# Regrouping v's projection weights on GpSimd, and projecting v by full-width matmuls

## The chip, the core and the metric

The kernel runs on one core of one Trainium2 chip, with one launch. The time is that of the device, in microseconds; a result is the median of several executions. Engines are named as in the profile: PE (TensorE, with PEld for its weight loads), DVE (VectorE), ACT (ScalarE), POOL (GpSimd) and SP (SyncE, which here only issues DMAs).

## The reference

Two independent parts are computed on 2048 tokens of width 576, and laid side by side in the output. Part A is a local attention with 32 heads of 18 elements and a window of 8 positions, 2 apart. Part B is a gated long convolution (short taps on k, times v, a convolution as long as the sequence, times q).

```python
# part A
qkv = (x @ wqkv).reshape(B, S, 3, H, Dh)               # H = 32, Dh = 18
logits = einsum("bhsd,bhswd->bhsw", q, kg) * scale     # kg, vg: k, v at s - 2w, w = 0..7
o = einsum("bhsw,bhswd->bhsd", softmax(logits), vg)
a = o.reshape(B, S, D) @ wo
# part B
kv = (sum over t of k_pad[t:t + S] * shift_k[:, 3 - t]) * v
b = q * (irfft(rfft(kv) * rfft(ssm_k)) + kv * ssm_D)
```

## The kernel before

**Layout.** Part A works with features on the partitions. `project(comp, jj)` makes q, k and v (comp 0, 1, 2) from the transposed x: output features in four tiles of 128 (ct 0 to 3) and one of 64 (ct 4), tokens in two halves of 1024 (jj). The 576 input features are contracted as four blocks of 128 (`body`, kb 0 to 3, lines 360 and 364) and a tail of 64 (`tails`, lines 371 and 377). One unit of work is a tile for 512 of its tokens; two units fill a two-bank PSUM tile, which ACT evacuates (line 394).

**The order of v's features.** q and k are wanted in the order of the weights. v and the attention output are wanted in another: feature a + 9 n of the matrix (a = 0 to 8, n = 0 to 63) stands in row n of group a, so that a column tile holds two groups a of 64 features. Head h has features 18 h to 18 h + 17, so row n then belongs to head n // 2, which lets softmax weights be spread over partitions by one DMA. The kernel gets this order when it loads weights into PE: `wa(kb, a)` is a view of 64 columns of v's weights with a step of 9 elements. Each of them makes a matmul over 64 columns of the array, and two of these, at column positions 0 and 64, fill one PSUM tile.

**The work around it.** VectorE first makes the taps of part B for four blocks of 512 tokens (`taps`, lines 558 to 562), while PE projects q and k, folds finished blocks (`mirror`, line 570) and folds the filter (`fold_filter`, line 615). Then come the logits (DVE products line 745, head sums on PE line 754), softmax (lines 773 to 789), the weighted sums of v (line 846 and PE line 862 or 876), and the output projection; the spectra of part B (lines 589 and 692) are filled in between, and its products and inverse transform (lines 985, 1006, 1038) end the kernel.

**What sets the order.** The program is scheduled by hand. Matmul work lies in a queue `units`; at marked points `until()` takes the next few, a count from the list `PLACES`, so that PE's order is fixed when the kernel is built, with the help of a planner's clocks (`pe`, `dve`) that use constants. v's nine units are interleaved with the spectra of x by the list `FXS`. Every engine takes its instructions in their order.

**Places the change touches.** `xw` holds the transposed x and the weights; `w_at` says where. `Ks` is a large scratch tile that holds angles of the sine tables early on and filter spectra later. `load_w` issues three DMAs of one third of wqkv on SP's queue: one of 512 rows, and two of the last 64, once for each half of the partitions. It already takes another target in `to`. The third for v is loaded in the loop over the taps at i = 1, between the filter's transposing loads. POOL builds constants at the start (lines 212 to 295), and later issues DMAs, among them those of `fold_filter` (line 620).

Of the kernel before, what the change touches and what calls it, by code (L numbers as in the profile page):

```python
# [31 lines left out]
def view(t, offset, dims):  # L32

    return bass.AP(tensor=t.tensor, offset=t.offset + offset, ap=[list(t.ap[0])] + [list(d) for d in dims])
# [3 lines left out]
def kernel(  # L38
# [13 lines left out]
    nc = tc.nc  # L52
    Bsz, S, D = A_x.shape
# [42 lines left out]
    def bank2(name, tag):  # L96
        return pp.tile([128, 2, 512], FP32, name=name, tag=tag)
# [6 lines left out]
    xw = main.tile([128, 12 * HB], BF16, name="xw")  # L104
# [11 lines left out]
    def xT(kb, t0, n):  # L116
        return view(xw, HB * (3 + 3 * (t0 // 1024)) + 1024 * kb + t0 % 1024, [[1, n]])

    def x5(jj):
        return view(xw, HB * (3 + 3 * jj) + 4096, [[1, 512]])  # L120

    def w_at(kb, comp):
        return HB * (9, 10, 5)[comp] + D * kb if kb < 4 else 11 * HB + D * (1, 2, 0)[comp]

    def wq(kb, comp, c0, n):
        return view(xw, w_at(kb, comp) + c0, [[1, n]])

    def wa(kb, a):

        return view(xw, w_at(kb, 2) + a, [[9, 64]])  # L130

    def load_w(eng, comp, to=None):
        low, high = (to[:, 0:4, :], to[:, 4, :]) if to is not None else \
            (view(xw, w_at(0, comp), [[D, 4], [1, D]]), wq(4, comp, 0, D))
        eng.dma_start(low, A_wqkv[0:512, comp * D:(comp + 1) * D].rearrange("(kb p) a -> p kb a", p=128))
        for r in range(2):
            eng.dma_start(high[64 * r:64 * r + 64, :], A_wqkv[512:576, comp * D:(comp + 1) * D])
# [25 lines left out]
    Ks = main.tile([128, 12 * HB], BF16, name="Ks")  # L163
# [3 lines left out]
    def k_at(m, part):  # L167
        return 3 * HB * (3 - m) + HB * part

    def kTok(m):  # L170
        return view(Ks, k_at(m, 2), [[D, 4], [1, D]])
# [24 lines left out]
    def load_v(i):  # L196
        vt = sp1.tile([128, 4, D], BF16, name="vt", bufs=2)
        nc.sync.dma_start(vt[0:128:2], vf[BL * i:BL * i + 256, :].rearrange("(p c) d -> p c d", c=4))
        nc.sync.dma_start(vt[1:128:2], bass.AP(tensor=vf.tensor, offset=vf.offset + (BL * i + 256 + 3) * D,
                                              ap=[[4 * D, 64], [-D, 4], [1, D]]))  # L200
        vts.append(vt)

    def load_filter(m):

        m = NBL - 1 - m
        nc.sync.dma_start_transpose(kTok(m), B_ssm_k[:, BL * m:BL * m + BL])
# [62 lines left out]
    for c0, p0, p1 in ((0, 0, 128), (128, 0, 128), (256, 0, 128), (384, 0, 128), (512, 0, 64), (512, 64, 128)):  # L269
        EHS.append(main.tile([128, 32], BF16, name=f"E{len(EHS)}"))  # L270
        e = EHS[-1][p0:p1, :]
# [43 lines left out]
    def pe(us, tag, evac, ready=0.0, first=True, last=True):  # L315

        clk["P"] = max(clk["P"], ready, psum[tag].popleft() if first else 0.0) + us
        clk["A"] = max(clk["A"], clk["P"] + 0.1) + evac
        if last:
            psum[tag].append(clk["A"])  # L320
        return clk["A"]
# [8 lines left out]
    def until():  # L330

        for _ in range(next(places, 0)):
            if units:
                p = max(clk["P"], psum["A"][0] if psum["A"] else 0.0)
                pop(next((n for n, u in enumerate(units) if len(u) < 4 or u[3] <= p), 0))
# [13 lines left out]
    def dest(comp, ct):  # L349
        if comp == 0:  # L350
            return q, (ct * S if ct < 4 else 4 * S), 0
        return (k if comp == 1 else v), (ct * KW if ct < 4 else 4 * KW), PAD


    def project(comp, jj):
        def body(ps, ct, jj, jp, first):
            for kb in range(4):
                se = dict(start=(kb == 0 and not first), stop=(kb == 3 and first))
                if ct < 4 and comp < 2:
                    nc.tensor.matmul(ps[:, jp, :], wq(kb, comp, 128 * ct, 128), xT(kb, 1024 * jj + 512 * jp, 512), **se)  # L360
                    continue
                for e in range(2):
                    w = wa(kb, min(2 * ct + e, 8)) if comp == 2 else wq(kb, comp, 512, 64)
                    nc.tensor.matmul(ps[64 * e:64 * e + 64, jp, :], w, xT(kb, 1024 * (jj if ct < 4 else e) + 512 * jp, 512),  # L364
                                     tile_position=(0, 64 * e), **se)

        def tails(ps, ct, jj, first):
            se = dict(start=first, stop=not first)
            if ct < 4 and comp < 2:
                for r in range(2):  # L370
                    nc.tensor.matmul(ps[:, r, :], wq(4, comp, 128 * ct, 128)[64 * r:64 * r + 64],  # L371
                                     x5(jj)[64 * r:64 * r + 64], tile_position=(64 * r, 0), **se)
                return
            for e in range(2):
                w = wa(4, min(2 * ct + e, 8)) if comp == 2 else wq(4, comp, 512, 64)
                for r in range(2):
                    nc.tensor.matmul(ps[64 * e:64 * e + 64, r, :], w[64 * r:64 * r + 64],  # L377
                                     x5(jj if ct < 4 else e)[64 * r:64 * r + 64], tile_position=(64 * r, 64 * e), **se)

        def unit(ct, jj, jp, first, box):  # L380
            t, o, pad = dest(comp, ct)
            if jp == 0:
                box["ps"] = bank2("ps_proj", "A")
                if first:
                    tails(box["ps"], ct, jj, True)
            ps = box["ps"]
            body(ps, ct, jj, jp, first)
            if jp == 0:
                clk["P"] += 1.15 if first else 0.9
                return  # L390
            if not first:
                tails(ps, ct, jj, False)
            pe(0.9 if first else 1.15, "A", 1.02)
            nc.scalar.activation(view(t, o + pad + 1024 * jj, [[512, 2], [1, 512]]), ps[:], ACT.Copy)  # L394
            if ct == 4 and comp > 0:
                nc.scalar.dma_start(view(t, o, [[1, PAD]])[64:128, :], view(t, o + 1024, [[1, PAD]])[0:64, :])

        for ct in range(4) if jj < 2 else [4]:
            first = ct % 2 == 1 if ct < 4 else comp == 1
            box = {}  # L400
            for jp in range(2):
                units.append((0.9 + 0.25 * (jp != first), partial(unit, ct, jj % 2, jp, first, box),
                              f"v{jj}{ct}" if comp == 2 else f"proj{comp}"))
# [149 lines left out]
    def taps(i):  # L553
        kj, vt = kjs[i], vts[i]
        kv = kv_of(i)
        for j in (3, 2, 1, 0):
            o = kv if j == 3 else sp1.tile([128, 4, D], BF16, name="tB")[:]
            dve(2304, lambda: nc.vector.tensor_tensor(  # L558
                o, kj[:, 3 - j:7 - j, :], skb[:, 3 - j, :].unsqueeze(1).to_broadcast([128, 4, D]), ALU.mult))
            if j < 3:  # L560
                dve(2304, lambda: nc.vector.tensor_tensor(kv, kv, o, ALU.add))  # L561
        return dve(2304, lambda: nc.vector.tensor_tensor(kv, kv, vt[:], ALU.mult))
# [85 lines left out]
    def add_half(t, to, of):  # L648
        nc.gpsimd.dma_start(half(t, to), half(t, of), accum_op=ALU.add, max_dma_last_dim=HB)

    def turn_filter(m):
        for part in range(2):
            add_half(Ks, k_at(m, part), k_at(m - 1, part))

    for i in range(NBL):
        r = taps(i)
        until()
        if i < 2:
            load_k(i + 2)
            load_v(i + 2)  # L660
        if i == 1:
            load_filter(0)
            load_w(nc.sync, 2)
            for m in range(1, NBL):
                load_filter(m)
        if i == 1:
            nc.scalar.preload_act_table_set("natural_log_exp_and_others")
            nc.scalar.activation(warm[:], pib[:], ACT.Exp)
        rest = [units.popleft()] if i == 3 and units and getattr(units[0][1], "args", ())[2:3] == (1,) else []
        for n in range(2):  # L670
            units.insert(3 * n, (0.5, partial(mirror, i, n), "x"))
        if i == 3:
            units.extendleft([fold_filter(m) for m in (3, 2)][::-1] + rest)
# [456 lines left out]
    for n, (j, t, i) in enumerate(todo):  # L1130
# [5 lines left out]
        if i == j and t == 2 and j < NBL - 1:  # L1136
            a, b = inverse(j, 0, HD, r), inverse(j, HD, HD, r)
# [40 lines left out]
```

## Time and profile before

| | |
|---|---|
| time, median of 3 runs | 221.6 us (221.13 to 221.75) |
| the profiled execution | 221.13 us, of which the span is 219.4 us |
| PE busy | 206.3 us (94%) |
| DVE busy | 200.3 us (91%) |
| ACT busy | 151.6 us (69%) |
| POOL busy | 48.9 us (22%) |
| granted PE clock | full speed in all but the last stretch (0.99) |

Times of single instructions are counted from the start of the span. A row of a timeline gives start, length, engine, line, operation, output and input, and count of merged instructions; a bracket says how long the engine had idled before it and what ended that. PE's matmuls overlap, so a group's length in the chain of waits says more than the sum of its matmuls.

### The profile page before, as it was taken

Reading aid. Unit: us, or ns where it says so; the run is one execution under the profiler, and the core shown is the slowest. Engines: PE = TensorE matmul, PEld = TensorE weight load, DVE = VectorE, ACT = ScalarE, POOL = GpSimd, SP = SyncE. Lnnn points to the kernel's source line nnn. Section 1 sums busy time; section 2 is a strip of 40 time slices with the busy share of each in tenths; the row PEclk is TensorE's granted clock in tenths of the full one; section 3 lists DMA queues with packets and bytes.
Section 4 is the critical chain, followed back from the end, with each engine's and each line's share of the span. In section 5 each row is a group of like instructions: output and inputs, shape, how many; then the busy total and the mean of one; then the engine's idle time right before and its main releaser. Section 6 shows DMA issues by size and latency. Waiting matters only on the chain.

```text
span 219.4 us, 5341 instructions
## 1 busy us (share of the span) xinstructions
PE 206.3 (94%) x2262; PEld 119.1 (54%) x2266; DVE 200.3 (91%) x159; ACT 151.6 (69%) x218; POOL 48.9 (22%) x93
## 2 busy tenths in 40 slices
PE   7999899999699999999999999999979999999891
PEld 3543344444455556565576777555546666666560
DVE  7969999999989949899898699999999999999982
ACT  3699766896686799965359888755487776756530
POOL 8989800000320206220640000000240001130000
PEclk9999999999999999999999999999999999999999
DMA  6999987999150035999999485481282103580034
GB/s 211 269 282 276 266 286 253 158 200 253 28 87 4 0 54 82 189 178 221 226 249 236 59 232 133 68 183 55 74 249 74 40 4 108 172 251 13 3 100 115
DMA packets 32295, 32.59 MB, mean 149 GB/s; under 512 B 17136, under 2 KB 28016, under 8 KB 32272
## 3 DMA queue, kind: packets, MB, share of 16 engines
q1 hardware_dynamic: 25902, 21.93, 41.2%
q0 software_dynamic: 3744, 7.82, 17.8%
q10 hardware_dynamic: 2626, 2.52, 3.4%
q8 instruction: 17, 0.28, 0.5%
q14 instruction: 6, 0.05, 0.1%
HBM read 13.11 MB, written 4.72 MB: 81 GB/s over the span
## 4 chain that ended last, share of the span: by engine, by line
PE 72%; ACT 15%; DVE 7%; issue 3%; DVEq 0%; ACTq 0%
PE ps_proj L364 10%; PE ps_proj L360 7%; PE ps_acc L862 7%; PE ps_wo L915 6%; PE ps_z L1006 6%; PE ps_inv L1038 5%; PE ps_fx L692 4%; PE ps_log L754 4%; PE ps_fk L589 3%; PE ps_proj L482 3%; ACT Ks L635 2%; ACT xw L695 2%; PE ps_rev L615 2%; ACT qk L394 2%; PE ps_proj L377 2%
## 5 line engine op out<-in xcount | busy, mean ns | idle before, releaser
L745 DVE TENSOR_TENSOR av<-qk 128x4096 bf16<-128x4096 bf16 (+1 forms) x20 | 40.5, 2074 | 4.3 <-PE ps_log L754 4.2
L360 PE MATMUL ps_proj<-xw 128*128 128x512 bf16 x93 | 22.6, 380 | 0.8 <-ACT qk L394 0.5
L364 PE MATMUL ps_proj<-xw 128*64 128x512 bf16 x176 | 23.0, 396 | 0.0
L1019 ACT ACTIVATE av<-ps_z 128x768 bf16<-128x768 f32 x23 | 17.4, 809 | 5.3 <-PE ps_z L1006 5.3
L695 ACT ACTIVATE xw<-ps_fx 128x576 bf16<-128x576 f32 x32 | 18.5, 665 | 2.0 <-PE ps_fx L692 2.0
L974 POOL DMA_DIRECT2D TB<-in_B_q_dram x4 | 3.0, 742 | 75.7 <-DVE qk L846 45.4
L635 ACT ACTIVATE Ks<-ps_fk 128x576 bf16<-128x576 f32 x32 | 18.3, 660 | 1.7 <-PE ps_fk L590 1.5
L394 ACT ACTIVATE qk<-ps_proj 128x1024 bf16<-128x1024 f32 x14 | 14.4, 1027 | 7.0 <-PE ps_proj L371 3.7
L364 PEld LDWEIGHTS <-xw 128*64 128x64 bf16 x176 | 14.7, 180 | 7.3 <-issue 5.2
L915 PE MATMUL ps_wo<-qk 128*128 128x288 bf16 x128 | 18.1, 287 | 0.4 <-ACT qk L866 0.4
L692 PE MATMUL ps_fx<-xw,TB 64*128 64x288 bf16 x256 | 17.8, 283 | 0.2 <-ACT xw L571 0.2
L589 PE MATMUL ps_fk<-Ks,TB 128*128 128x384 bf16 x64 | 17.2, 327 | 0.1
L394 ACT ACTIVATE v<-ps_proj 128x1024 bf16<-128x1024 f32 x9 | 9.2, 1025 | 11.4 <-PE ps_proj L377 7.0
L561 DVE TENSOR_TENSOR xw<-xw,tB 128x2304 bf16<-128x2304 bf16 x12 | 16.3, 1358 | 0.4
L1038 PE MATMUL ps_inv<-av,TI 128*128 128x288 bf16 (+1 forms) x112 | 16.1, 292 | 0.6 <-ACT av L1019 0.6
L558 DVE TENSOR_TENSOR tB<-kj,skb 128x2304 bf16<-128x2304 bf16 x12 | 16.3, 1356 | 0.3
L620 POOL DMA_DIRECT2D Ks<-Ks x4 | 5.0, 1242 | 50.8 <-ACT Ks L618 50.8
L590 PE MATMUL ps_fk<-Ks,TB 128*128 128x192 bf16 x64 | 15.7, 246 | 0.0
L692 PEld LDWEIGHTS <-TB 64*128 64x128 bf16 x256 | 12.1, 94 | 6.5 <-issue 4.3
L922 ACT ACTIVATE qk<-ps_wo 128x576 bf16<-128x576 f32 x16 | 10.4, 650 | 7.3 <-PE ps_wo L907 4.5
L862 PE MATMUL ps_acc<-av,ident 64*64 64x512 bf16 x160 | 15.3, 378 | 0.1
L1041 ACT ACTIVATE v<-ps_inv 128x576 bf16<-128x576 f32 (+1 forms) x14 | 9.5, 675 | 8.3 <-PE ps_inv L1038 8.3
(187 smaller groups left out, 455.2 us busy)
## 6 DMA issues: line engine op xcount, KB each, us to landing
kj<-in_B_k_dram SPq DMA_DIRECT2D x7, 504.0 KB, 5.4
Ks<-Ks POOLq DMA_DIRECT2D x6, 576.0 KB, 8.3
TB<-av SPq DMA_DIRECT2D x12, 256.0 KB, 5.2
vt<-in_B_v_dram SPq DMA_DIRECT2D x8, 288.0 KB, 4.3
out_dram<-qk ACTq DMA_DIRECT2D x8, 288.0 KB, 2.4
Ks<-av SPq DMA_DIRECT2D x8, 256.0 KB, 5.1
xw<-in_A_wqkv_dram SPq DMA_DIRECT2D x3, 576.0 KB, 5.6
Ks<-in_A_x_dram SPq DMA_DIRECT2D x2, 576.0 KB, 5.2
```

The costliest lines, as they stand in the source:

```text
L360: nc.tensor.matmul(ps[:, jp, :], wq(kb, comp, 128 * ct, 128), xT(kb, 1024 * jj + 512 * jp, 512), **se)
L364: nc.tensor.matmul(ps[64 * e:64 * e + 64, jp, :], w, xT(kb, 1024 * (jj if ct < 4 else e) + 512 * jp, 512), tile_position=(0, 64 * e), **se)
L394: nc.scalar.activation(view(t, o + pad + 1024 * jj, [[512, 2], [1, 512]]), ps[:], ACT.Copy)
L589: nc.tensor.matmul(o[:, 0:2], w, rhs[:, 0:2], start=start, stop=stop)
L635: nc.scalar.activation(view(Ks, k_at(m, cs ^ (m & 1)) + 96 * gi, [[768, 3], [384, 2], [1, 96]]), acc3(ps), ACT.Copy, scale=(PSG, MSG)[cs][ ...
L692: nc.tensor.matmul(ps[:, pm, 0:HD], TX[64 * pm:64 * pm + 64, c, 128 * gi:128 * gi + 128], kv[64 * pm:64 * pm + 64, c, HD * h:HD * h + HD], ...
L695: nc.scalar.activation(view(xw, HB * XG[i] + 96 * gi + 1152 * h, [[HB, 2], [384, 3], [1, 96]]), view(ps, 0, [[512, 2], [96, 3], [1, 96]]), ...
L745: r = dve(1024 * nj, lambda: nc.vector.tensor_tensor(view(prod, 0, [[256 * nj, 4], [256, nj], [1, 256]]), view(t, o + 256 * hh, [[0, 4], [ ...
L862: nc.tensor.matmul(acc[64 * o:64 * o + 64, h, :], ident[64 * h:64 * h + 64, 64 * h:64 * h + 64], view(P, 256 * u, [[2048, 2], [1, 256]])[6 ...
L915: nc.tensor.matmul(ps[:, r, 0:HD], oT(hh, j + 2 * r, t)[:, o:o + 128], wo[:, t // 2, t % 2, HD * h:HD * h + HD], start=(t == 0 and h == 0) ...
L1019: nc.scalar.activation(y, z, ACT.Copy)
L1038: nc.tensor.matmul(ps[:, c, 0:n], TI[:, sl, pm, 128 * c:128 * c + 128], Yall[:, j % 2, pm, sl, c0:c0 + n], start=(pm == 0 and sl == 0), st ...
```

## The change

The load of v's weights goes to a stretch of `Ks` (`raw`), as they lie in DRAM. Five copies on GpSimd, one for each block of input features, read each block with a step of 9 elements and write it packed to where the weights stood before, group a by group a. `project` then treats v as q and k for its four full tiles: one matmul of 128 columns takes the place of two of 64, and two tail matmuls that of four. The fifth tile, of 64 features, keeps its two column positions and reads the packed weights. `wa` is gone, which moves the lines behind it up by four.

```diff
-    def wa(kb, a):
-
-        return view(xw, w_at(kb, 2) + a, [[9, 64]])
...
         def body(ps, ct, jj, jp, first):
             for kb in range(4):
                 se = dict(start=(kb == 0 and not first), stop=(kb == 3 and first))
-                if ct < 4 and comp < 2:
+                if ct < 4:
                     nc.tensor.matmul(ps[:, jp, :], wq(kb, comp, 128 * ct, 128), xT(kb, 1024 * jj + 512 * jp, 512), **se)
                     continue
                 for e in range(2):
-                    w = wa(kb, min(2 * ct + e, 8)) if comp == 2 else wq(kb, comp, 512, 64)
+                    w = wq(kb, comp, 512, 64)
...
         def tails(ps, ct, jj, first):
             se = dict(start=first, stop=not first)
-            if ct < 4 and comp < 2:
+            if ct < 4:
                 for r in range(2):
                     nc.tensor.matmul(ps[:, r, :], wq(4, comp, 128 * ct, 128)[64 * r:64 * r + 64],
                                      x5(jj)[64 * r:64 * r + 64], tile_position=(64 * r, 0), **se)
                 return
             for e in range(2):
-                w = wa(4, min(2 * ct + e, 8)) if comp == 2 else wq(4, comp, 512, 64)
+                w = wq(4, comp, 512, 64)
...
+    raw = view(Ks, k_at(0, 0), [[D, 5], [1, D]])
+
     for i in range(NBL):
         r = taps(i)
         until()
...
         if i == 1:
             load_filter(0)
-            load_w(nc.sync, 2)
+            load_w(nc.sync, 2, raw)
             for m in range(1, NBL):
                 load_filter(m)
+            for kb in range(5):
+                nc.gpsimd.tensor_copy(view(xw, w_at(kb, 2), [[64, 9], [1, 64]]), view(raw, D * kb, [[1, 9], [9, 64]]))
```

## The prediction

> **What bounds the kernel now.** I read the page first: busy times, and the shares of the chain that ended last.
>
> ```profile
> span 219.4 us, 5341 instructions
> PE 206.3 (94%) x2262; PEld 119.1 (54%) x2266; DVE 200.3 (91%) x159; ACT 151.6 (69%) x218; POOL 48.9 (22%) x93
> PE 72%; ACT 15%; DVE 7%; issue 3%; DVEq 0%; ACTq 0%
> ```
>
> TensorE and VectorE are both nearly full, so an average says nothing; the stage decides. Next, the busy time of each engine by stretches.
>
> ```profile
> 95.00:110.00 15.00, 15.00 (x152) 8.23 (x152) 13.94 (x8) 7.08 (x10) 4.34 (x8) 1.00 1.00 212
> 110.00:124.00 14.00, 14.00 (x182) 9.61 (x180) 11.40 (x12) 10.53 (x14) 2.19 (x2) 1.00 0.88 199
> 124.00:160.00 36.00, 35.30 (x495) 22.39 (x493) 35.92 (x20) 24.25 (x36) 2.40 (x4) 1.00 0.52 123
> ```
>
> The columns after the length are busy PE, weight loads, DVE, ACT, POOL, then granted clock and DMA. From 95 to 124 us, where v is projected, PE has no gap and DVE idles for 3.7 us; from 124 on DVE is full. The timeline of DVE says who makes it wait, and where it stops waiting.
>
> ```profile
> 62.87 14.44 DVE L745 TENSOR_TENSOR av<-qk 128x4096 bf16<-128x4096 bf16 x7 [1.06 <-PE ps_log L754]
> ...
> 122.63 1.23 DVE L789 TENSOR_TENSOR av<-av,xw 128x2048 bf16<-128x2048 bf16 x1 [1.74 <-ACT xw L787]
> 123.77 4.49 DVE L846 TENSOR_TENSOR av<-Ks,v 128x4096 bf16<-128x4096 bf16 x2
> ```
>
> The last wait is at 122.63: the second softmax's multiply waits for an Exp, which stands in ScalarE's queue behind evacuations that wait for PE. After it DVE runs without a gap to the tail. So whatever PE saves before that point starts the DVE-bound rest sooner, and whatever delays PE or DVE before it delays everything.
>
> **What is removed: half-width matmuls.** The chain in order of time (start, length, line, count) has both kinds. L364 and L377 are the 64-column products of v and their tails; L360 and L371 are those of q and k at full width. One of v's units is 16 products now and 8 afterwards, 4 tails now and 2 afterwards. A unit comes whole (x16) or as two halves (x8) with other work between; below stand the first and last of its six halves and five wholes ahead of 124 us, and the twins of q and k.
>
> ```profile
> 96.04 1.07 PE ps_proj L364 x8
> 98.72 0.42 PE ps_proj L377 x4
> 100.11 1.93 PE ps_proj L364 x16
> 105.27 0.64 PE ps_proj L377 x8
> 107.52 1.07 PE ps_proj L364 x8
> 122.25 1.95 PE ps_proj L364 x16
> ...
> 36.82 0.97 PE ps_proj L360 x4
> 47.62 1.83 PE ps_proj L360 x8
> 47.30 0.32 PE ps_proj L371 x2
> 36.28 0.54 PE ps_proj L371 x4
> ```
>
> A half or a whole is shortened by 0.10 us (1.07 to 0.97, 1.93 to 1.83), a single set of tails by 0.10, a joined pair of sets by 0.10 (0.64 to 0.54). The two column halves already run side by side, so this is all there is. Before the decisive wait at 122.63 lie six halves, four of the five wholes (that at 122.25 comes too late), three single and two joined tails: 15 x 0.10 = 1.5 us. PE is gapless there, so I book all of it: **-1.5 us**. Bounds: none of it, if the strip pairs' cost returns in another form; 1.9 with the last unit, rounding, and the ninth unit, which stays half-width but reads packed weights. Evacuations, their order and the sizes in the planner are untouched, so no unit changes place on any queue.
>
> **What is moved: the load.** Three DMAs keep their place on SP's queue and their bytes; only the target is Ks instead of xw. That part of Ks held angles of the sine tables; the last sine in the chain, and when the load is issued:
>
> ```profile
> 22.48 1.04 ACT TB L422
> ```
> ```profile
> 42.33 0.59 SPq L135 DMA_DIRECT2D xw<-in_A_wqkv_dram  x1
> xw<-in_A_wqkv_dram SPq DMA_DIRECT2D x1, 576.0 KB, 4.6
> ```
>
> The new wait is over 19 us before the issue: it costs nothing, and the filter transposes queued behind it on SP are not held.
>
> **What is added: five copies on GpSimd**, 576 elements per partition each, reading with a step of 9 elements. They wait on POOL for the load, which lands (last column of the second row) 4.6 us after its issue: 42.33 + 4.6 = 46.9 us. DVE is then in the taps of block 3, back to back.
>
> ```profile
> 46.22 1.35 DVE L558 TENSOR_TENSOR xw<-kj,skb 128x2304 bf16<-128x2304 bf16 x1
> 47.48 1.35 DVE L558 TENSOR_TENSOR tB<-kj,skb 128x2304 bf16<-128x2304 bf16 x1
> 48.87 1.36 DVE L561 TENSOR_TENSOR xw<-xw,tB 128x2304 bf16<-128x2304 bf16 x1
> ...
> 55.83 1.36 DVE L562 TENSOR_TENSOR xw<-xw,vt 128x2304 bf16<-128x2304 bf16 x1
> 57.32 4.49 DVE L745 TENSOR_TENSOR av<-qk 128x4096 bf16<-128x4096 bf16 x2
> ```
>
> How do POOL and DVE get on? Earlier, the same taps ran beside copies and multiplies by a constant on POOL.
>
> ```profile
> 17.49 1.36 DVE L558 TENSOR_TENSOR tB<-kj,skb 128x2304 bf16<-128x2304 bf16 x1
> 18.89 1.36 DVE L561 TENSOR_TENSOR xw<-xw,tB 128x2304 bf16<-128x2304 bf16 x1
> 23.06 1.36 DVE L562 TENSOR_TENSOR xw<-xw,vt 128x2304 bf16<-128x2304 bf16 x1
> 24.34 1.44 DVE L558 TENSOR_TENSOR xw<-kj,skb 128x2304 bf16<-128x2304 bf16 x1
> ```
> ```profile
> 17.67 1.33 POOL L284 COPY flip<-flip 128x128 bf16<-128x128 bf16 x1
> 23.39 1.42 POOL L295 TENSOR_SCALAR identn<-ident 128x128 bf16<-128x128 bf16 x1
> ```
>
> The copy of 17.67 ends at 19.00, 0.15 us after the DVE operation of 17.49 ends (18.85); L295 ends at 24.81, 0.39 after that of 23.06 (24.42). POOL's readers wait for the end of a DVE operation: one gets through per operation. Then it is DVE's turn to be held: the operation at 24.34 takes 1.44 where its like at 46.22 takes 1.35, so 128 elements held it by 0.09. The operation at 18.89 lost nothing, because it depends on its forerunner and starts 1.39 after it where an independent one starts 1.26 after (46.22 to 47.48): 0.12 of slack hides a short reader. Copies of 576 elements do not fit into that.
>
> The trace has no POOL reader of that length or step, so I bound the stall of one copy. Low end: 0.09 x 576/128 = 0.40 us, a packed read. High end: L295's 0.39 x 4.5 = 1.76 us, if DVE is held until POOL is done. Zero or a gain is excluded only by the single row at 24.34, so zero stays as a rival. I take the middle, 1.1 us: the low end's reads are packed and these are not, the high end's operation is dearer than a copy and its record includes the write. [...] No run here shows a strided read yet.
>
> Five copies take five slots, the first between the operations of 46.22 and 47.48 (no slack), the others with 0.12: DVE ends its taps later by 5 x 1.1 - 0.5 = **5.0 us**. POOL is through by about 47.6 + 5 x 1.1 + 4 x 1.35 = 58.5 us.
>
> Who is waiting behind? On POOL, the accumulating DMA of the filter fold, and v's pads:
>
> ```profile
> 57.76 1.33 POOL L620 DMA_DIRECT2D Ks<-Ks  x1 [31.37 <-ACT Ks L618]
> 62.15 1.05 PE L754 MATMUL ps_log<-av,E 128*32 128x512 bf16 x16
> 68.03 1.07 PE ps_proj L364 x8
> ```
>
> The DMA goes out under 1 us late, and its readers on PE come later still. The first product of v comes at 68.03, 9 us after the copies. What does not hide is DVE's lateness: the fold of block 3 needs its taps, the first logits its products, and PE takes its instructions in order. The second half of the row at 62.15 starts near 62.65 and needs the two products that end at 57.32 + 4.49 = 61.81: 0.84 of cover. Beyond that PE has no other work in its order and moves back with DVE: 5.0 - 0.8 = **+4.2 us**. (DVE's own idle 1.06 at 62.87 gives nothing more, as PE is then the later one.)
>
> **Sum**: 4.2 - 1.5 = +2.7 us. The profiled execution took 221.13 us (span 219.4 and 1.73 around it), so 223.8; that run is the fastest of three with a median of 221.6, so 0.5 more for a median: **224.3 us**.
>
> **Rivals.**
>
> *The copies slip in and the kernel is faster.* If a copy costs DVE less than 0.43 us, DVE is late by less than 1.7, of which 0.84 is covered, and the shorter PE stage wins by over 0.3%; at no stall, -1.5 us: 220.1. For it: the rows at 18.89 and 23.06, unmoved, and L295, whose 0.39 past the release cost DVE only 0.09. Against it: the row at 24.34, and reads 4.5 times as long with a step.
>
> *They cancel.* Between 0.43 and 0.70 us a copy, for instance 0.55, DVE is 2.3 us late, PE 1.4 to 1.5, and the gain eats that: 221.6.
>
> *DVE is held for a copy's whole length.* From 1.4 us up, to 1.76: 8.3 us late, +6.0, 227.6. For it: POOL's readers wait until the DVE operation is entirely over, so the reverse may hold. [...]
>
> *It is not what it says:* the wide products are no faster on their own turn. Then the 1.5 us are missing, which moves each case up; it is inside the upper range.
>
> **How the numbers follow.** The forecast, 0.7 to 1.4 us a copy, gives +0.7 to +4.2, that is 222.3 to 225.8: chance 0.50. Full holding 0.14, cancelling 0.14, slipping in 0.22. About 0.3% (0.66 us) is what a measurement of this kernel can tell from no change. So slower 0.64, same 0.14, faster 0.22. The range, 219.9 to 226.8, reaches to no stall and into part of the full holding.
>
> **What would show it.** In the timeline of the changed kernel: five copies on POOL between 47 and 60 us, one per DVE operation; the taps of block 3 ending near 62 instead of 57.2, each held operation longer by about 1 us; PE idle for some 4 us ahead of the folds of block 3, named after DVE; v's groups x8 at 1.83 and x4 at 0.97. I am wrong if DVE's operations there keep 1.36 us, or if PE's gap opens and the end does not move.

## The result, and the profile after

The changed kernel is slower: 225.0 us, the median of 4 runs (224.57 to 225.93), against 221.64 us (221.13 to 221.75) for the kernel before in the same rounds. The ratio is 1.0162, with a 95% interval of 1.0124 to 1.02. The profiled execution took 225.29 us with a span of 223.6 us, so the span grew by 4.2 us.

First the head of the page after, the two strips of TensorE (busy share and granted clock, 40 slices of 5.6 us), the shares of the chain that ended last, and the group of the new copies.

```profile
span 223.6 us, 5189 instructions
PE 207.3 (93%) x2186; PEld 112.2 (50%) x2186; DVE 204.9 (92%) x159; ACT 152.0 (68%) x218; POOL 60.4 (27%) x98
...
PE   7999999999379999999999999999979999999891
PEclk9999999999958999999999999999999999999998
...
PE 50%; DVE 25%; ACT 9%; DMA 6%; SPq 5%; issue 4%; DVEq 0%; ACTq 0%
...
L665 POOL COPY xw<-Ks 128x576 bf16<-128x576 bf16 x5 | 11.2, 2289 | 19.2 <-DMA Ks<-in_A_wqkv_dram 19.2
```

DVE's share of the chain went from 7% to 25%, PE's from 72% to 50%; but the kernel with the gain alone, below, has 23% and 54%, so these shares don't show what the copies do. The strips do better. The eleventh slice has a hole in PE (3, where it was 6 before), and in the twelfth and thirteenth the granted clock falls (5 and 8), which it did not do there before. DVE does the same 159 operations in 4.6 us more. A copy's record of 2289 ns is more than twice what it holds a tap for (0.91 to 1.04 us, below); I put the rest down to its own wait for DVE. The timelines of DVE and POOL show the two side by side.

```profile
46.63 2.39 DVE L554 TENSOR_TENSOR xw<-kj,skb 128x2304 bf16<-128x2304 bf16 x1
48.95 2.40 DVE L554 TENSOR_TENSOR tB<-kj,skb 128x2304 bf16<-128x2304 bf16 x1
51.38 2.29 DVE L557 TENSOR_TENSOR xw<-xw,tB 128x2304 bf16<-128x2304 bf16 x1
53.71 2.29 DVE L554 TENSOR_TENSOR tB<-kj,skb 128x2304 bf16<-128x2304 bf16 x1
56.03 2.27 DVE L557 TENSOR_TENSOR xw<-xw,tB 128x2304 bf16<-128x2304 bf16 x1
58.34 1.36 DVE L554 TENSOR_TENSOR tB<-kj,skb 128x2304 bf16<-128x2304 bf16 x1
...
61.12 1.36 DVE L558 TENSOR_TENSOR xw<-xw,vt 128x2304 bf16<-128x2304 bf16 x1
...
126.89 1.23 DVE L789 TENSOR_TENSOR av<-av,xw 128x2048 bf16<-128x2048 bf16 x1 [1.76 <-ACT xw L787]
128.03 4.49 DVE L846 TENSOR_TENSOR av<-Ks,v 128x4096 bf16<-128x4096 bf16 x2
```
```profile
45.86 11.23 POOL L665 COPY xw<-Ks 128x576 bf16<-128x576 bf16 x5 [19.16 <-DMA Ks<-in_A_wqkv_dram]
57.92 1.33 POOL L616 DMA_DIRECT2D Ks<-Ks  x1 [0.83 <-ACT Ks L614]
```

Exactly five taps of block 3 are long, one for each copy: 2.39, 2.40, 2.29, 2.29 and 2.27 us, where the next, with no copy left, takes 1.36. Against 1.36 they are held by 1.03, 1.04, 0.93, 0.93 and 0.91, together 4.84 us. The first two depend on nothing just ahead of them, the other three on their forerunners, and these lose 0.11 less. Now PE, by its timeline and by stretches; the last row is a stretch of the kernel before.

```profile
62.53 1.12 PE L566 MATMUL ps_fold<-xw,fold 128*128 128x288 bf16 x4 [3.78 <-DVE xw L558]
65.28 2.10 PE L692 MATMUL ps_fx<-xw,TB 64*128 64x288 bf16 x16 [0.20 <-ACT xw L567]
68.81 1.15 PE L692 MATMUL ps_fx<-xw,TB 64*128 64x288 bf16 x16
```
```profile
60.00:62.00 2.00, 0.00 (x0) 0.00 (x0) 1.97 (x2) 0.00 (x0) 1.98 (x4) 0.89 1.09 153
62.00:64.00 2.00, 1.21 (x5) 0.64 (x5) 1.87 (x2) 0.80 (x2) 0.00 (x0) 0.50 0.85 126
64.00:66.00 2.00, 1.80 (x12) 0.89 (x13) 2.00 (x2) 1.59 (x3) 0.00 (x0) 0.50 0.01 2
...
68.00:70.00 2.00, 2.00 (x29) 0.97 (x22) 1.53 (x1) 0.57 (x2) 0.00 (x0) 0.90 0.02 1
```
```profile
64.00:66.00 2.00, 2.00 (x22) 1.14 (x20) 2.00 (x2) 2.00 (x5) 0.00 (x0) 1.00 0.01 1
```

PE waits 3.78 us for the last tap. Then comes something that the prediction does not have: when the work arrives, PE runs at a granted clock of 0.50 until a little after 68 us. The same 16 matmuls of the spectra take 2.10 us at 65.28 and 1.15 at 68.81. Before the change the clock was 1.00 here.

Last, the chain in order of time in v's stage:

```profile
101.47 0.97 PE ps_proj L356 x4
105.19 1.83 PE ps_proj L356 x8
110.05 0.54 PE ps_proj L367 x4
122.72 0.32 PE ps_proj L367 x2
```

They are the lengths of q and k, as forecast: a half 0.97 instead of 1.07, a whole 1.83 instead of 1.93, tails 0.54 and 0.32 instead of 0.64 and 0.42. The gain is there, and what was lost ahead of it is larger.

### The profile page after: what moved, and what is told of

The parts are those of the page before. It is cut to its first block, busy times and chain, and to the rows that moved or that the text cites. A ratio compares the mean times of both kernels' runs of the same rounds, so it can differ in the third digit from the quotient of the medians.

```text
span 223.6 us, 5189 instructions
## 1 busy us (share of the span) xinstructions
PE 207.3 (93%) x2186; PEld 112.2 (50%) x2186; DVE 204.9 (92%) x159; ACT 152.0 (68%) x218; POOL 60.4 (27%) x98
## 4 chain that ended last, share of the span: by engine, by line
PE 50%; DVE 25%; ACT 9%; DMA 6%; SPq 5%; issue 4%; DVEq 0%; ACTq 0%
PE ps_acc L862 7%; DVE xw L557 6%; DVE tB L554 6%; PE ps_wo L915 6%; PE ps_proj L356 6%; PE ps_z L1006 6%; PE ps_inv L1038 5%; PE ps_log L754 5%; PE ps_fx L692 4%; PE ps_fk L585 3%; DMA kj<-in_B_k_dram 3%; DMA Ks<-in_A_x_dram 3%; SPq L229 3%; ACT Ks L631 2%; DVE xw L554 2%
## 5 line engine op out<-in xcount | busy, mean ns | idle before, releaser
L356 PE MATMUL ps_proj<-xw 128*128 128x512 bf16 x160 | 38.8, 380 | 0.5 <-ACT qk L390 0.5
L356 PEld LDWEIGHTS <-xw 128*128 128x128 bf16 x160 | 14.0, 97 | 20.8 <-issue 7.3
L692 PE MATMUL ps_fx<-xw,TB 64*128 64x288 bf16 x256 | 18.7, 293 | 0.2 <-ACT xw L567 0.2
L554 DVE TENSOR_TENSOR tB<-kj,skb 128x2304 bf16<-128x2304 bf16 x12 | 18.3, 1522 | 0.3
L557 DVE TENSOR_TENSOR xw<-xw,tB 128x2304 bf16<-128x2304 bf16 x12 | 18.1, 1511 | 0.4
L665 POOL COPY xw<-Ks 128x576 bf16<-128x576 bf16 x5 | 11.2, 2289 | 19.2 <-DMA Ks<-in_A_wqkv_dram 19.2
L915 PEld LDWEIGHTS <-qk 128*128 128x128 bf16 x128 | 11.4, 98 | 6.6 <-issue 3.0
```

The lines of the kernel that those rows point to most:

```text
L554: dve(2304, lambda: nc.vector.tensor_tensor(o, kj[:, 3 - j:7 - j, :], skb[:, 3 - j, :].unsqueeze(1).to_broadcast([128, 4, D]), ALU.mult))
L692: nc.tensor.matmul(ps[:, pm, 0:HD], TX[64 * pm:64 * pm + 64, c, 128 * gi:128 * gi + 128], kv[64 * pm:64 * pm + 64, c, HD * h:HD * h + HD], ...
L915: nc.tensor.matmul(ps[:, r, 0:HD], oT(hh, j + 2 * r, t)[:, o:o + 128], wo[:, t // 2, t % 2, HD * h:HD * h + HD], start=(t == 0 and h == 0) ...
```

## The experiments

Theory L: a GpSimd copy and a tap on DVE exclude each other for the copy's whole length. Rival S: DVE is held only as long as the copy reads, and the step of the read made that long. Beside these stands the question of what the low clock costs. All ratios are to the kernel before on the same chip. The copies alone, the stepped write, PE kept at work and the regrouping by ScalarE ran on one chip (before: 221.08 us), the other kernels on a second (before: 221.11 us).

| kernel | median us | ratio, 95% interval | DVE start after the second softmax |
|---|---|---|---|
| before | 221.1 | 1 | 123.77 |
| after, run again | 225.11 | 1.0162 (1.0126 to 1.0197) | 128.05 |
| copies alone | 226.57 | 1.0237 (1.0213 to 1.0261) | 129.30 |
| gain alone | 219.28 | 0.9912 (0.9887 to 0.9937) | 122.29 |
| packed read, stepped write | 228.75 | 1.0351 (1.0321 to 1.0381) | 131.21 |
| packed read and write | 220.84 | 0.9991 (0.9971 to 1.0011) | 123.54 |
| after, PE kept at work | 223.71 | 1.0121 (1.0104 to 1.0138) | 126.46 |
| regrouped by ScalarE | 220.58 | 0.9983 (0.9973 to 0.9994) | 123.27 |
| regrouped by DVE in its gaps | 219.83 | 0.995 (0.9931 to 0.9969) | 123.21 |

The last column is the start of the row "av<-Ks,v ... x2" that was at 123.77 before. The spans move with it: in each of these kernels the change of the span is within 0.15 us of the change of this start. So the prediction's reading, that everything up to there decides and the rest only follows, holds for all of them. These starts are those of one profiled execution each, the medians those of all.

**Copies alone.** The kernel before with the five copies added; they go to the part of Ks that nobody reads then, and v is projected as before.

```diff
+            for kb in range(5):
+                nc.gpsimd.tensor_copy(view(Ks, k_at(0, 0) + D * kb, [[64, 9], [1, 64]]),
+                                      view(xw, w_at(kb, 2), [[1, 9], [9, 64]]))
```

> The kernel before, its half-width matmuls on v's weights as they lie, and beside them five GpSimd copies of these weights with the same step of 9 elements to a place that nothing reads. Theory (the copies hold VectorE, and the shorter matmuls give back 1.4 us): the whole loss of the copies without the gain, 221.6 + 4.9 of held taps - 0.8 of cover + about 1.2 for PE's half clock = 226.9 us (226 to 228), five taps of block 3 at about 2.3 us. Rival (the loss lies in the new matmuls or in the load's new target): as before, 221.6 us within 0.5, whatever the taps do.

Measured: 226.57 us, 5.5 more than before. Timeline of DVE, first held tap, last tap, and the start that decides; and one stretch of the windows:

```profile
46.15 2.39 DVE L558 TENSOR_TENSOR xw<-kj,skb 128x2304 bf16<-128x2304 bf16 x1
60.62 1.36 DVE L562 TENSOR_TENSOR xw<-xw,vt 128x2304 bf16<-128x2304 bf16 x1
129.30 4.49 DVE L849 TENSOR_TENSOR av<-Ks,v 128x4096 bf16<-128x4096 bf16 x2
```
```profile
64.00:66.00 2.00, 1.80 (x15) 1.05 (x15) 2.00 (x2) 1.23 (x3) 0.00 (x0) 0.50 0.01 1
```

The taps end at 61.98 instead of 57.19, 4.79 late. Less the 0.84 of cover that is 3.95, but the decisive start is 5.53 late. The missing 1.6 us lie between, where PE's clock is 0.50. The new matmuls and the load's new target are not in this kernel, so the loss is that of the copies, and it has two parts.

**Gain alone.** The changed kernel without copies: the load goes where the weights are read, so that v's features stand in another order; the regrouping is left out.

```diff
-            load_w(nc.sync, 2, raw)
+            load_w(nc.sync, 2)
...
-            for kb in range(5):
-                nc.gpsimd.tensor_copy(...)
```

> The changed kernel without regrouping: v's weights are loaded to their place as they lie and used full-width in that order, so v's features are in another order; the same number of instructions of the same shape, no copies on any engine. Theory: the gain alone, 221.1 - 1.45 = 219.6 us (219.2 to 220.1), with DVE's last wait ahead of the second softmax's multiply that much earlier. Rival (full-width brings nothing to the end): 221.1.

Measured: 219.28 us, 1.83 less than before. Timeline of DVE:

```profile
122.29 4.49 DVE L844 TENSOR_TENSOR av<-Ks,v 128x4096 bf16<-128x4096 bf16 x2
```

It starts 1.48 us earlier than before, where the prediction counted 1.5. The medians give somewhat more, 1.83, in part because the profiled execution, 219.55 us, lies 0.27 above its kernel's median.

**After, run again**, on the chip of the gain alone.

> The changed kernel itself, on the chip of these runs, beside which the clock's share is read: 221.1 x 1.0162 = 224.7 us (224.2 to 225.2). The theory of the clock gives it a granted clock of 0.98 and 1.0 to 1.4 us more than with the filler; the rival, within 0.4 us of that.

Measured: 225.11 us, so the copies cost 225.11 - 219.28 = 5.8 us where the gain is taken too, and 5.5 where it isn't: gain and loss about add up. The executions spread from 223.65 to 225.57 us.

**Packed read, stepped write.** The same elements, walked in the other order: the read is packed, and the write goes with a step of 64 elements.

```diff
-                nc.gpsimd.tensor_copy(view(xw, w_at(kb, 2), [[64, 9], [1, 64]]), view(raw, D * kb, [[1, 9], [9, 64]]))
+                nc.gpsimd.tensor_copy(view(xw, w_at(kb, 2), [[1, 64], [64, 9]]), view(raw, D * kb, [[9, 64], [1, 9]]))
```

> The changed kernel with the copies turned round: they read packed (576 elements in a row) and write with a step of 64, to the same result. Theory S (VectorE is held as long as the copy reads, and the read's step of 18 bytes made it long): the hold falls from 0.97 to 0.4 to 0.5 us a copy, taps late by some 2.2 us, no half clock, 221.6 + 2.2 - 0.8 - 1.4 = 221.6 us (221.0 to 222.3). Theory L (VectorE is held for the copy's whole length, which the element count sets): holds as with the strided read, 225.0 us (224.3 to 226). A strided write slower than the strided read would give more than 226 under L, and change nothing under S.

Measured: 228.75 us. Timeline of DVE (a tap without and one with dependency slack, and the last held one) and of POOL:

```profile
46.45 3.30 DVE L554 TENSOR_TENSOR xw<-kj,skb 128x2304 bf16<-128x2304 bf16 x1
53.01 3.19 DVE L557 TENSOR_TENSOR xw<-xw,tB 128x2304 bf16<-128x2304 bf16 x1
...
59.43 3.15 DVE L557 TENSOR_TENSOR xw<-xw,tB 128x2304 bf16<-128x2304 bf16 x1
```
```profile
45.76 16.25 POOL L665 COPY xw<-Ks 128x576 bf16<-128x576 bf16 x5 [19.33 <-DMA Ks<-in_A_wqkv_dram]
```

S as it was put falls: with a packed read the taps are held longer, by 1.94 and 1.83 us each. L's number, 225.0, is missed as well; only its added clause came true, that a write slower than the read would give over 226. So the element count doesn't set a copy's length (16.25 us for the five records here, 11.23 in the changed kernel), and this step in the write is dearer than that in the read (1.94 against 1.04).

**Packed read and write.** One step further: both sides packed, which leaves the regrouping out.

```diff
+                nc.gpsimd.tensor_copy(view(xw, w_at(kb, 2), [[64, 9], [1, 64]]), view(raw, D * kb, [[64, 9], [1, 64]]))
```

> The changed kernel with five copies of the same size on GpSimd that read packed and write packed, so the regrouping is left out (v's features stand in another order). It measures the hold of 576 elements without a step. Theory L (VectorE is held for the copy's whole length, and a step, in the read or in the write, makes the copy long): 0.4 to 0.6 us a copy, taps late by 2 to 2.5 us, 221.1 + 2.2 - 0.8 - 1.45 = 221.0 us (220.4 to 221.6). Rival (the element count alone sets it): 0.97 us a copy, as in the changed kernel.

Measured: 220.84 us. Timeline of DVE and POOL:

```profile
46.16 1.82 DVE L554 TENSOR_TENSOR xw<-kj,skb 128x2304 bf16<-128x2304 bf16 x1
49.75 1.70 DVE L557 TENSOR_TENSOR xw<-xw,tB 128x2304 bf16<-128x2304 bf16 x1
53.22 1.70 DVE L557 TENSOR_TENSOR xw<-xw,tB 128x2304 bf16<-128x2304 bf16 x1
```
```profile
45.90 7.81 POOL L665 COPY xw<-Ks 128x576 bf16<-128x576 bf16 x5 [19.55 <-DMA Ks<-in_A_wqkv_dram]
```

The same 576 elements hold a tap by 0.46 or 0.34 us. With both sides packed, five copies are almost exactly paid for by the wide matmuls. So the three kernels give what a copy holds a tap for, without slack: 0.46 packed, 1.04 with a read step of 9 elements (18 bytes), 1.94 with a write step of 64 (128 bytes).

Is that the copy's whole length? The last copy's record tells. It ends at 57.09 in the changed kernel (45.86 + 11.23), at 53.71 here and at 62.01 with stepped writes. The tap beside it ends at 58.30, 54.92 and 62.58; less its own 1.36 us, DVE was let go at 56.94, 53.56 and 61.22. That is 0.15 us before the copy's record ends in the first two kernels, but 0.79 with stepped writes. So L fits where the writes are packed. With stepped writes DVE goes on while the copy's record still runs, as far as the records of POOL, which are rough, can tell. A hold that lasts as long as the copy reads would fit all three only if its reads wait for its writes; no run shows whether they do.

**After, PE kept at work.** The changed kernel with 16 matmuls of 512 columns, whose result nobody reads, put on PE between the filter's folds and the folds of block 3.

```diff
+    def filler():
+        ps = bank2("ps_idle", "A")
+        for _ in range(16):
+            nc.tensor.matmul(ps[:, 0, :], ident[:], xT(0, 0, 512), start=True, stop=True)
...
-            units.extendleft([fold_filter(m) for m in (3, 2)][::-1] + rest)
+            units.extendleft([(0.0, filler, "x")] + [fold_filter(m) for m in (3, 2)][::-1] + rest)
```

> The changed kernel with 16 matmuls that nobody reads in PE's gap ahead of block 3's folds (16 x 0.22 = 3.5 us of the 3.78 us gap). It leaves the holds as they are and only keeps PE at work. Theory (the gap also halved PE's clock from 61 to 68 us, which cost 1.2 us more): the granted clock stays at 1.00, and the time falls from 225.0 to 223.8 us (223.4 to 224.3). Rival (PE was waiting for VectorE anyhow, and the half clock cost nothing): 225.0 us within 0.4 at a clock of 1.00.

Measured: 223.71 us, 2.63 above its kernel before, where the changed kernel run again is 4.00 above its own on the other chip: 1.4 us less by the medians, 0.9 by the two ratios of the table. Timeline of PE, then the windows, then DVE's last tap:

```profile
58.69 3.61 PE L656 MATMUL ps_idle<-xw,ident 128*128 128x512 bf16 x16 [0.25 <-ACT Ks L614]
62.14 0.65 PE L566 MATMUL ps_fold<-xw,fold 128*128 128x288 bf16 x4
```
```profile
62.00:64.00 2.00, 1.37 (x10) 0.71 (x8) 1.87 (x2) 1.41 (x3) 0.00 (x0) 1.00 0.84 123
64.00:66.00 2.00, 1.80 (x26) 1.10 (x25) 2.00 (x2) 1.79 (x4) 0.00 (x0) 1.00 0.01 1
```
```profile
60.66 1.36 DVE L558 TENSOR_TENSOR xw<-xw,vt 128x2304 bf16<-128x2304 bf16 x1
```

The clock stays at 1.00, and the folds start 0.12 us after the taps end (62.02); in the changed kernel they started 0.05 after (62.53 and 62.48), so the added matmuls bring them no sooner. The prediction's sum now comes out: taps 4.83 us late, less 0.84 of cover, less 1.5 of gain, is +2.5; the decisive start is 2.69 late. The packed copies, whose gap in PE is 0.62 us and whose clock stays at 1.00, give the same picture: taps 1.91 late, sum -0.43, start -0.23. So the low clock after the gap, not some other cost of the copies, is what the sum lacked.

How long does the low clock last? The mean clock of a stretch gives the moment at which it changed: 0.89 in 60 to 62 us means that half speed began at 61.56, and 0.90 in 68 to 70 that it ended at 68.4, after 6.84 us. The windows of the changed kernel's second profile, and of the kernel with stepped writes:

```profile
62.00:64.00 2.00, 1.51 (x8) 0.71 (x7) 1.96 (x1) 1.41 (x3) 0.00 (x0) 0.64 0.54 78
68.00:70.00 2.00, 2.00 (x21) 1.00 (x18) 2.00 (x2) 0.47 (x1) 0.00 (x0) 0.65 0.01 1
```
```profile
62.00:64.00 2.00, 0.00 (x0) 0.00 (x0) 1.95 (x2) 0.00 (x0) 2.00 (x3) 0.87 0.27 40
70.00:72.00 2.00, 2.00 (x32) 0.99 (x28) 1.67 (x2) 1.25 (x3) 0.00 (x0) 0.92 0.02 1
```

They give 62.56 to 69.4 and 63.48 to 70.32: 6.84 us each time, whenever PE's work began. When the clock fell, PE had been idle for 2.8 us in the changed kernel's profile (58.75 to 61.56), for 4.3 in its second (58.21 to 62.56) and for 4.9 with stepped writes (58.54 to 63.48), so the three show no fixed length of idle time ahead of it. Since the low time was 6.84 us in all three, what it costs depends on where the work falls. In the profile of the changed kernel, PE works from 62.53 to 68.4 at half speed, and the decisive start is 1.3 us later than the taps' lateness (5.29), the cover and the gain explain. In its second profile the folds start 0.57 us sooner (61.96), but the low clock lasts a microsecond longer, to 69.4, and the decisive start comes no sooner (128.05): there the low clock costs 1.9. With stepped writes PE's work begins at 66.8, when half of the low time is over: there the taps (9.58 late) explain +7.24 of +7.44.

**Regrouped by ScalarE.** The five copies go to ACT, after the 8th, 11th, 12th, 13th and 15th evacuation that follow the loading of v's weights.

```diff
+        kb = {8: 0, 11: 1, 12: 2, 13: 3, 15: 4}.get(ticks["n"])
+        if kb is not None:
+            nc.scalar.activation(view(xw, w_at(kb, 2), [[64, 9], [1, 64]]), view(raw, D * kb, [[1, 9], [9, 64]]), ACT.Copy)
```

> The changed kernel with the five copies on ScalarE, in gaps of its queue between 48 and 58 us, in place of GpSimd. Theory: no tap is held (all at 1.36 us), PE has no gap ahead of block 3's folds, and the gain of the full-width matmuls stands alone: 221.6 - 1.4 = 220.2 us (219.6 to 220.9). Rival A (full-width products bring nothing, because VectorE is the bound): 221.6. Rival B (ScalarE is on the chain from 54 to 61 us, and five copies of some 0.7 us push it): 221.5 to 223.

Measured: 220.58 us. DVE's taps keep 1.36. Timeline of ACT and PE, then PE's row of the kernel before:

```profile
57.78 1.39 ACT L136 ACTIVATE xw<-Ks 128x576 bf16<-128x576 bf16 x1
61.99 1.16 PE L704 MATMUL ps_fx<-xw,TB 64*128 64x288 bf16 x16 [0.20 <-ACT xw L578]
```
```profile
61.06 1.16 PE L692 MATMUL ps_fx<-xw,TB 64*128 64x288 bf16 x16 [0.20 <-ACT xw L571]
```

DVE goes free, and a copy takes 1.39 us instead of the 0.7 expected. ACT evacuates PSUM for PE here, and PE reaches its next spectra 0.93 us late; the decisive start is 0.98 later than with the gain alone. That eats most of the gain: the queue that looked free was feeding the bound. The forecast's range, 219.6 to 220.9, was met by luck: it was counted from 221.6, and against this chip's 221.08 the kernel wins 0.5 us, not 1.4. What shows is the mechanism of rival B, at a smaller price.

**Regrouped by DVE in its gaps.** No GpSimd and no ACT: six copies stand in DVE's order, ahead of the logits' third, tenth and eleventh product, where DVE waits for PE.

```diff
+    slots = {2: [(None, 0, 0)], 9: [((0, 1, 2), 0, 8)], 10: [((3,), 0, 8)]}
...
+                for s in slots.get(nlog[0], ()):
+                    regroup(*s)
```

> Full-width matmuls, with the regrouping on VectorE itself, as six copies in three places where VectorE waits for PE in the kernel before: ahead of the third logits product (idle 1.06 us; the five blocks' last group, needed first, and the tail block), ahead of the tenth (idle 2.12; three copies) and the eleventh (idle 0.62; one). Theory (the gain of 1.4 us is real, and the copies cost only what is not hidden): about 0.95, 1.8 and 0.6 us lie in these waits, taps and PE's clock stay as before, 221.1 - 1.4 = 219.7 us (219.2 to 220.3). Rival (the waits are not free, a copy there delays the next product's head sums on PE): 220.5 to 223 us.

Measured: 219.83 us, ratio 0.995 (0.9931 to 0.9969): the fastest kernel here that does the whole work, ahead of the kernels before and after the change. Timeline of DVE, then the row of the kernel before:

```profile
61.66 0.39 DVE L737 COPY xw<-Ks 128x256 bf16<-128x256 bf16 x1
61.98 1.22 DVE L733 COPY xw<-Ks 128x576 bf16<-128x576 bf16 x1
77.46 1.72 DVE L733 COPY xw<-Ks 128x512 bf16<-128x512 bf16 x3
79.41 1.22 DVE L760 TENSOR_TENSOR av<-qk 128x2048 bf16<-128x2048 bf16 x1 [0.23 <-PE ps_log L769]
```
```profile
79.43 1.22 DVE L745 TENSOR_TENSOR av<-qk 128x2048 bf16<-128x2048 bf16 x1 [2.12 <-PE ps_log L754]
```

Three copies of 512 elements take 1.72 us, and the product behind them starts at 79.41; before the change it started at 79.43 after 2.12 us of waiting. So DVE pays for them with time it did not use. Of the 1.83 us of the gain alone 1.3 are kept. The decisive start (123.21) is 0.92 later than with the gain alone. Of this, 0.30 is there after the first two copies (the third product starts at 63.11 instead of 62.81) and stays until 108.27 (0.28); the rest comes with a new wait of 0.55 us for a DMA at 113.76. But the profiled execution, 220.44, lies 0.61 above its kernel's median, so whether the median one has that wait stays open.

## Why the prediction was right

The forecast was 224.3 us in a range of 219.9 to 226.8, slower with 0.64; 225.0 was measured. Step by step:

- **The wide matmuls, -1.5 us.** Right. The gain alone moved the decisive start by 1.48 and the median by 1.83. The ninth unit, which went into the upper bound of 1.9 only, got shorter too: in the chain of the changed kernel its two halves take 0.98 (at 73.71 and 75.84) instead of 1.07 (at 68.03 and 70.24 before the change). It lies ahead of the decisive start, so it is no reason for the difference between the two figures; the slower profiled execution is one.
- **The load, at nothing.** Right: POOL's wait ends with the DMA at 45.86, 1 us sooner than reckoned, and no wait on the sine tables shows. The first copy still had to wait for the tap then running.
- **The stall of a copy, 1.1 us between 0.40 and 1.76.** Right in size: 1.04 without slack. The middle was chosen for the reason that held, that the reads are not packed; the low end, scaled from 128 packed elements, was near the packed copy's own 0.46. That a step of 18 bytes makes the read much dearer, the traces confirm (0.46 packed, 1.04 with it). They also show a dearer case, a longer step in the write (1.94).
- **The slack of 0.12 after a dependent operation.** Right: in the three kernels with GpSimd copies of different steps the dependent taps are held 0.10 to 0.16 less. But only three copies found it, not four, since the first two taps are independent.
- **DVE late by 5.0, and 0.84 of cover.** The taps ended at 62.48 instead of 57.19, 5.29 late, of which 0.41 were there already when block 3's first tap began (46.63, not 46.22). The second profile and the copies alone began without that delay, so it is no part of the mechanism; 4.9 is the change's share. The cover held, as the run with PE kept at work shows.
- **POOL's followers.** Right: the DMA at 57.92 instead of 57.76.
- **PE simply moves back with DVE, +4.2.** Here the sum failed. "PE idle for some 4 us" was in the text, and it came (3.78 us), but the step took PE's speed after the gap for given. The granted clock fell to 0.50 for 6.84 us, and this costs 0.9 to 1.4 us by the runs with PE kept at work. With it the sum is 5.29 - 0.84 - 1.5 + 0.9 to 1.4 = +3.85 to +4.35, and the span grew by 4.2. The term was at nothing in the prediction, without a reason.
- **The 0.5 for the median.** It went the other way: the profiled execution of after, 225.29, lies above its median by 0.29. For the profiled executions the sum gave +2.7 us and +4.2 was measured; the forecast of the median was off by only 0.7. That the number came out so much closer than its sum is luck.

Of the rivals, *slipping in* and *cancelling* would have needed copies as short as packed ones: that kernel, at 220.84, is in fact the case "they cancel". *DVE is held for a copy's whole length* was given 0.14 and an entry point of 1.4 us. That point, also the upper end of the forecast's 0.7 to 1.4 us, stands on no run of this case: the holds that the runs showed are 0.46, 1.04 and 1.94 us. As a mechanism it is nearly what happens where the writes are packed; the mistake was to tie it to a length that these copies don't have. With packed writes hold and record end within 0.15 us of each other, with stepped writes they don't (0.79). The row at 24.34 (held 0.09 beside a record of 0.39 past the release) is of the same kind, a record that goes on after DVE is let go, and stays open; the 0.09 itself is what the packed copy's 0.46 gives for 128 elements, 0.10 by proportion.

## What to carry to other kernels

A copy on an idle GpSimd was not free here beside DVE's taps: with 576 elements each held one by 0.46 us packed on both sides, 1.04 with the step in the read and 1.94 with that in the write. So count such a hold as DVE time, keep the copy packed on both sides, or put the work where DVE waits anyway (three copies of 512 elements on DVE, 1.72 us, moved the product behind them not at all: 79.41, and 79.43 before). When a change opens a gap ahead of the engine that bounds the stage, price what runs after the gap too: read the granted clock behind the nearest gap of that length, and if none is in the profile, carry what stood behind the gap of 3.78 us here, 0.50 for 6.84 us, as an estimate. A path with 0.84 us of cover and 1.5 us to win has room for 2.3 us of delay; over five copies that is 0.47 us each, which only the packed copies kept to (0.46 and 0.34).

## What the runs showed of the hardware that was not expected

- With a long write step a GpSimd copy cost more than with a short read step: it held DVE by 1.94 us for 576 elements with a step of 128 bytes in the write, 1.04 with 18 bytes in the read, 0.46 packed. Steps of equal size were not compared.
- PE's half clock behind the gap ahead of block 3's folds lasted 6.84 us by the windows of three profiles, whether PE had work from its start (folds from 61.96, low clock from 62.56) or only from its middle (66.82 of 63.48).
- ACT took 1.39 us for a copy of 576 elements from Ks to xw with the same read step; DVE took 0.57 for 512 (1.72 for three).
- DVE beside a GpSimd copy with stepped writes went on 0.79 us before the copy's record ended; beside copies with packed writes, 0.15.
